# Second expert's last four batches and the global rows moved into the Strassen part of an attention and mixture-of-experts kernel

## The chip, the cores and the metric

The kernel runs on one core of a Trainium2 chip. The metric is the device time of one execution in microseconds (us). The core has TensorE (PE: matmuls, and weight loads shown apart as PEld), VectorE (DVE), ScalarE (ACT), GpSimd (POOL) and SyncE (SP); POOL and SP issue the transfers (DMAs) of this kernel, each from its own queue in order. Every engine works through its own instructions in order.

## The reference

Eight batches, eight heads, 512 local and 32 global tokens, head width 64. Global tokens attend to everything; local ones attend to the 32 global keys and to local keys at a distance of at most 32. The result (4352 rows of 512) goes through eight experts, each two matrices with a ReLU between; each row's sum over the experts is weighted with a matrix P of rows by experts, made from the gate's logits by eight Sinkhorn iterations.

```python
s_g = scale * q_g @ k_all.T ; out_g = softmax(s_g) @ v_all
s_l = concat(scale * q_l @ k_g.T, where(|i - j| <= 32, scale * q_l @ k_l.T, -1e9))
out_l = softmax(s_l) @ concat(v_g, v_l)
x = concat(out_g, out_l) as rows of 512
P = exp(x @ w_gate - max)
for _ in range(8): P /= P.sum(1) ; P /= P.sum(0) ; P *= N / E
out = sum over e of P[:, e] * (relu(x @ w1[e]) @ w2[e])
```

w1 is 512 x 1024 and w2 is 1024 x 512 for every expert. The copies of x, weights and hidden values on the chip are in 16 bits, sums in 32.

## The kernel before

The rows are kept transposed in xT, in nine groups: the local rows of batch m are group m (0 to 7, 512 rows each), the global rows of all batches are group 8 (256 rows). The program has three parts.

**Attention with two experts' work in between** (loop at L516). A step s handles one pair of heads; four steps make a batch, 32 steps all eight, and steps 32 and 33 only finish. In a step TensorE runs, in the order written out from L580 on: scores in three pieces (`st_B`, L317), transposes of the exponentials (`st_D1`, `st_D2`), transposes of the next step's keys and queries (`st_A`, L297), the product with the values of the step before (`st_E`, L375), and in even and odd steps the first and the last parts of the global rows' attention (`st_G1` to `st_G3n`). Scores go through VectorE (mask and maximum, L344) to ScalarE (exponential, L347). The transposed queries are copied by ScalarE into qbd (L314), the keys by VectorE into kTe (L307). Each step's scores need the qbd that was copied in the step before.

Between these stand pieces of the first two experts, computed plainly. A first-layer piece `p_l1` (L468) is four matmuls of 128 x 512 (for group 8 of 128 x 256) and a ReLU by ScalarE or VectorE; a second-layer piece `p_l2` (L482) is eight matmuls and a copy by ScalarE, and after the last piece of a group SP stores the group's result in yd. `f1` and `f2` in the loop take the next piece of the step's lists l1 and l2, if there is one: a first-layer piece ahead of the scores' first part, two after their second part, one at the end of the step; a second-layer piece after `st_D1`, another after `st_E`. A step has four first-layer and two second-layer pieces, experts 0 and 1 in turn for each batch:

```python
pieces = range(4 * (s - 6) + 2, 4 * (s - 6) + 6)
l1 = [(i // FT % 2, i // FT // 2, i % FT) if i >= 0 else None for i in pieces]
```

In the same loop POOL makes sums of weight blocks for experts 2 to 7, which Strassen's scheme needs: `sums_load` (L100) loads a quarter of an expert's weights into pw, `sums_form` (L108) makes four sums with four operations on 16-bit values and stores them in DRAM (kept). From step 8 on there is one load a step, its sums a step later, 24 in all. POOL also issues the loads of queries, keys (L155) and values (L170 to L177) of the next batch; when the values are there, SP moves them and the batch's global values vgz (L161) into place.

**Sinkhorn.** The pieces that the loop didn't reach stand in `tail` (L669): the second layer of expert 1 for batch 6, and experts 0 and 1 for batch 7 and for group 8. They run between the Sinkhorn iterations (`tail_run`, by weight: 1 for a first-layer piece, 2 for a second-layer one). What is left by then is mixed into the first four slots of the third part (`fill` in `run_slot`, L953).

**Experts 2 to 7 by Strassen's scheme** (from L709), with 7 instead of 8 block products in both layers. Two halves (pas 0: batches 0 to 3; pas 1: group 8 and batches 4 to 7) go through the six experts, so there are 12 stages. A stage's first layer is in slots (class `Slot`): seven products, two matmuls of 512 columns each, for each of four slots per pair of batches, and for group 8 one slot with 56 matmuls of 128 columns. The second layer is in units (class `Unit`) of 28 matmuls of 256 columns. A slot's products are interleaved with those of the previous slot and of two units (`run_slot`). ScalarE and VectorE read, copy and add the products; VectorE makes the sums of hidden values (L806) and of tokens (`token_sum`, L739). `fetch` (L711) loads an expert's weights and the stored sums, over POOL's queue. The results of experts 0 and 1 come back from yd tile by tile and VectorE adds them (`stored_load`, `stored_add`). A stage with `e == 2` writes the accumulators first, by ScalarE (L849, L864); later ones add by VectorE. The last expert's second layer for the final units is plain (L870).

Of the kernel before, what the change touches and what calls it, by code (L numbers as in the profile page):

```python
# [23 lines left out]
def kernel(  # L24
# [13 lines left out]
    nc = tc.nc  # L38
# [54 lines left out]
    work = {}  # L93

# [33 lines left out]
    with ExitStack() as att:  # L128
# [379 lines left out]
        NU = B * HP  # L508
        nc.vector.tensor_copy(out=mask[:, 0, 0:KW], in_=mask[:, 1, 0:KW])
# [6 lines left out]
        for s in range(NU + 2):  # L516
# [32 lines left out]
            if 8 <= s < 8 + 4 * (E - 2):  # L549
                sums_load(s - 8)  # L550
            if 8 < s <= 8 + 4 * (E - 2):
                sums_form(s - 9)

            l1, l2 = [], []
            if s >= 5:
                pieces = range(4 * (s - 6) + 2, 4 * (s - 6) + 6)
                l1 = [(i // FT % 2, i // FT // 2, i % FT) if i >= 0 else None for i in pieces]
            if s >= 6:
                k, hf = divmod(s - 6, 2)
                if k >= 1:  # L560
                    l2 = [((k - 1) % 2, (k - 1) // 2, 2 * hf + i) for i in range(2)]
# [107 lines left out]
        tail = [(2, lambda c=c, **k: p_l2(1, B - 2, c, "a", **k)) for c in range(NJ)]  # L669
        for e, m in ((0, B - 1), (0, B), (1, B - 1), (1, B)):  # L670
            nt = groups[m][1] // P
            tail += [(1 if nt == NJ else 0.5, lambda e=e, m=m, fm=fm, **k: p_l1(e, m, fm, "a", **k))
                     for fm in range(2 if (e, m) == (0, B - 1) else 0, FT)]
            tail += [(2, lambda e=e, m=m, c=c, **k: p_l2(e, m, c, "a", **k)) for c in range(nt)]
# [25 lines left out]
    with tc.tile_pool(name="tpool", bufs=2) as tpool, \  # L700
# [8 lines left out]
        stages = [(pas, e) for pas in range(2) for e in range(2, E)]  # L709
        w1s, w2s, sws, vws, tbs, ogs = {}, {}, {}, {}, {}, {}  # L710
        def fetch(k, l):  # L711
# [7 lines left out]
            else:  # L719
# [4 lines left out]
                own = w[:, 0:HF, H2:D]  # L724
            for o, i in parts:
                nc.gpsimd.dma_start(out=o, in_=i)  # L726
            nc.gpsimd.dma_start(out=own, in_=kept[e][l][:, 3])
            nc.gpsimd.dma_start(out=s, in_=kept[e][l][:, 0:3])

# [61 lines left out]
        class Unit:  # L791
# [54 lines left out]
            def r2(self):  # L846
                z = self.z
                if self.e == 2:
# [12 lines left out]
            def r1(self):  # L861
                z = self.z[:, 2:4, :]
                if self.e == 2:
# [89 lines left out]
        def run_slot(a, jobs=()):  # L953
# [14 lines left out]
            if x is None:  # L968
                fill(1)
# [11 lines left out]
            if y is None:  # L981
                fill(some - 1)
# [36 lines left out]
        for k, (pas, e) in enumerate(stages):  # L1019
# [4 lines left out]
            if more:  # L1024
                jobs[0 if k else 4].append(lambda: fetch(k + 1, 0))
                jobs[5].append(lambda: fetch(k + 1, 1))
            else:
                jobs[5].append(lambda: work.__setitem__("last", load_w2(e)))
            if e == 2 and pas:
                for i in range(4):  # L1030
                    jobs[1 + i].append(lambda i=i: token_sum(3, i))
            if e == E - 1 and not pas:
                for i in range(4):
                    jobs[4 + i].append(lambda i=i: token_sum(2, i))
                    jobs[4 + i].append(lambda i=i: token_sum(NQ, i))
            if e == 2:
# [53 lines left out]
```

## Time and profile before

| | |
|---|---|
| median of 3 runs | 998.37 us (997.82 to 999.82) |
| profiled execution | 998.93 us |
| its span, first to last instruction | 997.2 us |
| mean granted TensorE clock | 0.998 |
| attention loop | to about 320 us |
| Sinkhorn iterations | 327 to 357 us |
| Strassen part | from 356 us |

Busy times are unions of an engine's instructions; matmuls overlap, each is shown with the time to its last result, so the distance between starts is what one costs. A row of the timeline has start, length, engine, line, operation, output and inputs, and how many were merged; brackets show idle time of the engine ahead of it and what ended it. In DMA rows the last number is the median time from issue to landing.

### The profile page before, as it was taken

Reading aid. Unit: us, or ns where it says so; the run is one execution under the profiler, and the core shown is the slowest. Engines: PE = TensorE matmul, PEld = TensorE weight load, DVE = VectorE, ACT = ScalarE, POOL = GpSimd, SP = SyncE. Lnnn points to the kernel's source line nnn. Section 1 sums busy time; section 2 is a strip of 40 time slices with the busy share of each in tenths; the row PEclk is TensorE's granted clock in tenths of the full one; section 3 lists DMA queues with packets and bytes.
Section 4 is the critical chain, followed back from the end, with each engine's and each line's share of the span. In section 5 each row is a group of like instructions: output and inputs, shape, how many; then the busy total and the mean of one; then the engine's idle time right before and its main releaser. Section 6 shows DMA issues by size and latency. Waiting matters only on the chain.

```text
span 997.2 us, 22451 instructions
## 1 busy us (share of the span) xinstructions
PE 982.5 (99%) x8868; PEld 641.0 (64%) x8868; DVE 767.2 (77%) x1858; ACT 655.5 (66%) x1342; POOL 301.7 (30%) x364
## 2 busy tenths in 40 slices
PE   7899999999999999999999999999999999999998
PEld 4566566656665555666666666676767676776764
DVE  7866665666653755889999888997899999888885
ACT  6888888888884566765555555557765555555551
POOL 9748887888850102111111111111111111100000
PEclk9999999999999999999999999999999999999999
DMA  9999999999952387554543333575664543123043
GB/s 167 186 156 199 239 206 221 222 200 222 234 144 85 108 241 169 161 147 121 122 107 74 75 75 74 128 214 129 165 148 117 117 96 66 53 65 74 2 106 127
DMA packets 138058, 138.68 MB, mean 139 GB/s; under 512 B 56608, under 2 KB 110048, under 8 KB 135904
## 3 DMA queue, kind: packets, MB, share of 16 engines
q0 software_dynamic: 105696, 87.32, 49.6%
q1 hardware_dynamic: 31696, 49.60, 15.5%
q8 instruction: 69, 1.13, 0.5%
q10 hardware_dynamic: 560, 0.33, 0.1%
q14 instruction: 37, 0.30, 0.1%
HBM read 144.46 MB, written 39.58 MB: 185 GB/s over the span
## 4 chain that ended last, share of the span: by engine, by line
PE 94%; POOL 3%; DMA 1%; DVE 1%; issue 0%; SPq 0%; ACT 0%; POOLq 0%; DVEq 0%
PE z L810 30%; PE pa L908 18%; PE py L489 12%; PE ph L475 12%; PE pb L908 9%; PE pc L908 4%; PE po L388 1%; PE ptw L354 1%; PE zp L879 1%; PE sc L337 1%; DMA vgz<-vg 1%; PE pk L305 1%; PE tgx L364 1%; PE pq L305 1%; PE sg L407 0%; POOL va L174 0%
## 5 line engine op out<-in xcount | busy, mean ns | idle before, releaser
L810 PEld LDWEIGHTS <-hs 128*128 128x128 f16 x2264 | 220.7, 98 | 91.8 <-DVE hs L806 0.4
L810 PE MATMUL z<-w2e,hs 128*128 128x256 f16 x1304 | 195.6, 273 | 0.0
L810 PE MATMUL z<-v,hs 128*128 128x256 f16 x960 | 144.0, 273 | 0.0
L475 PE MATMUL ph<-xT,w1e 128*128 128x512 f16 (+1 forms) x576 | 129.3, 367 | 0.6 <-ACT xT L372 0.6
L347 ACT ACTIVATE Pu<-ms,mx 128x160 f16<-128x160 f32 x256 | 120.1, 636 | 13.3 <-DVE mx L344 10.4
L489 PE MATMUL py<-w2e,hT 128*128 128x512 f16 x544 | 128.2, 379 | 0.0
L831 ACT COPY z<-z 128x256 f32<-128x256 f32 x98 | 35.0, 357 | 141.7 <-PE z L810 141.7
L908 PEld LDWEIGHTS <-w1e 128*128 128x128 f16 x960 | 87.1, 98 | 51.6 <-issue 1.0
L908 PE MATMUL pa<-t,s 128*128 128x512 f16 x384 | 114.2, 379 | 0.0
L726 POOL DMA_DIRECT2D w1e<-in_moe_w_dram x24 | 17.5, 734 | 297.5 <-PE pa L908 220.4
L344 DVE CUSTOM_DVE_ANT_0 ms<-sc,mask 128x160 f32<-128x160 f32 x256 | 70.2, 320 | 46.6 <-ACT yst L492 30.0
L844 DVE SCALAR_TENSOR_TENSOR oy<-z,lg,oy 128x512 f32<-128x512 f32 x128 | 95.8, 749 | 7.6 <-ACT oy L849 5.1
L806 DVE TENSOR_TENSOR hs<-hs 128x512 f16<-128x512 f16 x224 | 94.9, 424 | 8.2
L912 DVE CUSTOM_DVE_ANT_0 hx<-pb,s 128x512 f16<-128x512 f32 x96 | 65.9, 687 | 36.4 <-ACT s L942 30.2
L726 POOL DMA_DIRECT2D w2e<-in_moe_w_dram x24 | 19.8, 833 | 243.6 <-PE z L810 214.2
L928 ACT ACTIVATE hs<-pa 128x512 f16<-128x512 f32 x96 | 57.2, 596 | 47.0 <-PE pa L908 46.9
L475 PEld LDWEIGHTS <-w1e 128*128 128x128 f16 x576 | 53.4, 98 | 52.9
L912 DVE CUSTOM_DVE_ANT_0 hs<-pb,s 128x512 f16<-128x512 f32 x96 | 65.9, 686 | 24.1 <-ACT s L942 23.7
L908 PEld LDWEIGHTS <-s 128*128 128x128 f16 x720 | 65.6, 98 | 28.5 <-issue 0.3
L489 PEld LDWEIGHTS <-hT 128*128 128x128 f16 x544 | 49.8, 98 | 51.9
L480 DVE TENSOR_SCALAR hT<-ph 128x512 f16<-128x512 f32 x58 | 40.1, 692 | 55.1 <-PE ph L475 55.0
L478 ACT ACTIVATE hT<-ph 128x512 f16<-128x512 f32 (+1 forms) x86 | 50.6, 588 | 28.8 <-PE ph L475 28.4
(197 smaller groups left out, 1971.0 us busy)
## 6 DMA issues: line engine op xcount, KB each, us to landing
ys<-yd SPq DMA_DIRECT2D x68, 256.0 KB, 3.2
yd<-yst SPq DMA_DIRECT2D x16, 1024.0 KB, 5.9
pw<-in_moe_w_dram POOLq DMA_DIRECT2D x24, 512.0 KB, 10.1
kept<-psum POOLq DMA_DIRECT2D x24, 512.0 KB, 5.3
s<-kept POOLq DMA_DIRECT2D x12, 768.0 KB, 8.9
v<-kept POOLq DMA_DIRECT2D x12, 768.0 KB, 8.9
w1e<-in_moe_w_dram POOLq DMA_DIRECT2D x12, 512.0 KB, 5.3
w2e<-in_moe_w_dram POOLq DMA_DIRECT2D x12, 512.0 KB, 6.7
```

Source lines behind the costliest of these rows:

```text
L344: nc.vector.tensor_tensor_reduce(out=ms[:, ii, :], in0=sc[:, SW * ii : SW * (ii + 1)], in1=mask[:, mi, :], scale=-scale, scalar=BIG, op0=A ...
L347: nc.scalar.activation(out=d["Pu"][:, i // 4, :, i % 4], in_=ms[:, ii, :], func=AF.Exp, scale=-1.0, bias=d["mx"][:, i : i + 1])
L475: nc.tensor.matmul(ph[:, 0:n], wts[e][0][:, dk, P * fm : P * (fm + 1)], xT[:, dk, c0 : c0 + n], start=(dk == 0), stop=(dk == DP - 1))
L478: nc.scalar.activation(out=hT[:, fm, 0:n], in_=ph[:, 0:n], func=AF.Relu)
L480: nc.vector.tensor_scalar(out=hT[:, fm, 0:n], in0=ph[:, 0:n], scalar1=0.0, scalar2=None, op0=ALU.max)
L489: nc.tensor.matmul(py, hT[:, fk, P * c : P * (c + 1)], wts[e][1][:, fk, :], start=(fk == 0), stop=(fk == FT - 1))
L806: nc.vector.tensor_tensor(out=o, in0=x, in1=y, op=op)
L810: nc.tensor.matmul(o, lhs[:, fk, :], rhs[:, fk, :], start=(first and fk == 0), stop=(fk == HF - 1), skip_group_check=True)
L844: nc.vector.scalar_tensor_tensor(out=o, in0=z, scalar=p, in1=o, op0=ALU.mult, op1=ALU.add)
L908: nc.tensor.matmul(o, lhs[:, dk, P * f : P * (f + 1)], rhs[:, dk], start=(first and n == 0 and dk == 0), stop=(dk == HD - 1), skip_group_c ...
L912: nc.vector._custom_dve(TENSOR_ADD_SAT, out=self.to(i, j), in0=self.of(ps), in1=self.of(s), s0=BIG, s1=0.0)
L928: nc.scalar.activation(out=self.to(1, 0), in_=self.of(self.pa), func=AF.Relu)
```

## The change

Expert 1 is computed plainly only for batches 0 to 3. For batches 4 to 7 and group 8 it becomes a stage of its own in the second half, ahead of expert 2, so there are 13 stages; in that half expert 1 writes the accumulators first (`inits`), and only expert 0's stored results are added there.

The loop's pieces follow a new list of (expert, batch), `seq`, at 20 first-layer pieces in 7 steps (`done`), 80 in all, and half as many second-layer pieces, shifted by 8. Where a step has two or three first-layer pieces, the second place stays empty (`l1.insert(1, None)`). The tail has the second layer of expert 0 for batch 6, expert 0 for batch 7 and group 8, and expert 1 for batch 3. In the first slots the piece that stood ahead of a slot's first unit products when there was no unit yet is no longer drawn.

POOL makes and stores the weight sums of experts 2 to 6 only, 20 instead of 24, spread over steps 8 to 31 (`sum_slots`). For experts 1 and 7 `fetch` loads each matrix whole in one transfer, and VectorE makes the sums (`weight_sums`), 8 operations a matrix, spread over slots: those of the first layer in the stage before, in slots 2 to 7, those of the second layer in slots 0 to 3 of its own. The token sums of group 8 move one stage earlier.

```diff
+    KEPT = range(2, 7)
+    sum_slots = [8 + n * 25 // 20 for n in range(4 * len(KEPT))]
...
+        seq = [(0, 0), (1, 0), (0, 1), (0, 2), (1, 1), (0, 3), (0, 4), (1, 2), (0, 5), (0, 6)]
...
-            if 8 <= s < 8 + 4 * (E - 2):
-                sums_load(s - 8)
-            if 8 < s <= 8 + 4 * (E - 2):
-                sums_form(s - 9)
-
-            l1, l2 = [], []
-            if s >= 5:
-                pieces = range(4 * (s - 6) + 2, 4 * (s - 6) + 6)
-                l1 = [(i // FT % 2, i // FT // 2, i % FT) if i >= 0 else None for i in pieces]
-            if s >= 6:
-                k, hf = divmod(s - 6, 2)
-                if k >= 1:
-                    l2 = [((k - 1) % 2, (k - 1) // 2, 2 * hf + i) for i in range(2)]
+            if s in sum_slots:
+                sums_load(sum_slots.index(s))
+            if s - 1 in sum_slots:
+                sums_form(sum_slots.index(s - 1))
+
+            def done(s):
+                c = min(max((s - 5) * 20 // 7 + 2, 0), FT * len(seq)) if s >= 5 else 0
+                return c, max((c - FT) // 2, 0)
+
+            (p1, p2), (q1, q2) = done(s - 1), done(s)
+            l1 = [(*seq[i // FT], i % FT) for i in range(p1, q1)]
+            l2 = [(*seq[i // NJ], i % NJ) for i in range(p2, q2)]
+            if s == 5:
+                l1 = [None, None] + l1
+            if 1 < len(l1) < 4:
+                l1.insert(1, None)
...
-        tail = [(2, lambda c=c, **k: p_l2(1, B - 2, c, "a", **k)) for c in range(NJ)]
-        for e, m in ((0, B - 1), (0, B), (1, B - 1), (1, B)):
+        tail = [(2, lambda c=c, **k: p_l2(0, B - 2, c, "a", **k)) for c in range(NJ)]
+        for e, m in ((0, B - 1), (0, B), (1, 3)):
...
-        stages = [(pas, e) for pas in range(2) for e in range(2, E)]
+        stages = [(pas, e) for pas in range(2) for e in range(2 - pas, E)]
+        inits = [2] * NJ + [1] * (B + 1 - NJ)
...
+            if e not in KEPT:
+                nc.gpsimd.dma_start(out=w, in_=x)
+                return
...
+        def weight_sums(k, l):
+            if l == 0:
+                w, s = w1s[k], sws[k]
+                b11, b12, b21, b22 = (w[:, HD * i : HD * (i + 1), F // 2 * j : F // 2 * (j + 1)] for i in range(2) for j in range(2))
+                ops = ((s[:, 1], b11, b12, ALU.subtract), (b12, b12, b22, ALU.add),
+                       (s[:, 0], b12, b11, ALU.subtract), (s[:, 2], b21, s[:, 0], ALU.subtract))
+                parts = [slice(i, i + 1) for i in range(HD)]
+            else:
...
+            return [lambda o=o, x=x, y=y, op=op, r=r: nc.vector.tensor_tensor(out=o[:, r], in0=x[:, r], in1=y[:, r], op=op)
+                    for o, x, y, op in ops for r in parts]
...
-                if self.e == 2:
+                if self.e == inits[self.m]:
...
             do(a, "m1")
             some = -(-len(tail) // (HF - a.f)) if tail and a is not None else 0
-            if x is None:
-                fill(1)
             if a is not None and p is None:
                 fill(1)
                 some -= 1
...
             if y is None:
-                fill(some - 1)
+                fill(some)
...
+                if stages[k + 1][1] not in KEPT:
+                    for i, at in enumerate((2, 3, 4, 5, 6, 6, 7, 7)):
+                        jobs[at].append(lambda i=i: weight_sums(k + 1, 0)[i]())
...
+            if e not in KEPT:
+                for i in range(8):
+                    jobs[i // 2].append(lambda i=i: weight_sums(k, 1)[i]())
```

## Prediction

> **What bounds the kernel now.** I read the page first (busy time per engine), then busy time by windows for two attention steps and two stretches of the second part, then the timeline of one step, engine by engine, then transfers.
>
> ```profile
> PE 982.5 (99%) x8868; PEld 641.0 (64%) x8868; DVE 767.2 (77%) x1858; ACT 655.5 (66%) x1342; POOL 301.7 (30%) x364
> ...
> 202.48:212.85 10.37, 10.37 (x139) 6.29 (x138) 6.50 (x26) 8.32 (x17) 6.81 (x7) 1.00 1.22 270
> 212.85:222.94 10.09, 10.09 (x127) 6.15 (x126) 6.16 (x26) 8.76 (x19) 9.55 (x11) 1.00 0.86 152
> 550.00:575.00 25.00, 25.00 (x174) 16.76 (x172) 20.42 (x37) 14.24 (x30) 2.72 (x4) 1.00 0.33 75
> 625.00:650.00 25.00, 25.00 (x185) 17.23 (x183) 24.30 (x54) 14.25 (x29) 3.09 (x5) 1.00 0.55 138
> ```
>
> The first line is the page's; the others are windows (length, then busy time of PE, weight loads, DVE, ACT, POOL, then clock, DMA share, GB/s). The first window is step 22 of the attention loop, the second step 23. TensorE is busy from end to end at full clock, in attention as in the second part, so the time is TensorE's list of work. But in attention ScalarE has 8.3 to 8.8 of 10 us, and around 625 VectorE has 24.3 of 25: both become the bound if TensorE gets much shorter there.
>
> **TensorE's own list.** These rows give its prices and the length of a stage.
>
> ```profile
> 205.95 1.89 PE L475 MATMUL ph<-xT,w1e 128*128 128x512 f16 x8
> ...
> 649.85 1.45 POOL L726 DMA_DIRECT2D w1e<-in_moe_w_dram  x2 [19.21 <-PE pa L908]
> 704.66 1.45 POOL L726 DMA_DIRECT2D w1e<-in_moe_w_dram  x2 [24.95 <-PE pa L908]
> ```
>
> Eight 512-column matmuls start at 205.95 and the next work at 207.67: 0.216 us each. A 256-column one takes 0.109 (four of L810 in 0.43). Removed for the second expert: per batch 32 matmuls in each layer, 4 x 64 x 0.216 = 55.3; global rows 32 x 0.109 + 16 x 0.216 = 6.9; together 62.2 us. Added: one more second-half stage. Its length is the distance between two weight fetches, 704.66 - 649.85 = 54.8 us. Balance: **-7.4 us**, if nothing waits.
>
> Of the 62.2, attention (steps 5 to 33) gives up 57.0: 34 first-layer pieces (114 to 80) of 0.864 and 16 second-layer pieces (52 to 36) of 1.73. The pieces behind the loop give up 5.2, all among those mixed into the first four slots: the Sinkhorn iterations draw about the same weight of pieces as before. What covered other engines' latency is gone there, so I walk the places.
>
> **ScalarE's turn in a step.** These ACT rows are from step 22 (its first score matmul is at 202.48); between the first two stand a global row's exponential and three copies.
>
> ```profile
> 203.39 1.37 ACT L347 ACTIVATE Pu<-ms,mx 128x160 f16<-128x160 f32 x3
> ...
> 206.79 1.39 ACT L347 ACTIVATE Pu<-ms,mx 128x160 f16<-128x160 f32 x3
> 207.90 0.70 ACT L478 ACTIVATE hT<-ph 128x512 f16<-128x512 f32 x1
> 208.84 1.01 ACT L347 ACTIVATE Pu<-ms,mx 128x160 f16<-128x160 f32 x2 [0.24 <-DVE mx L344]
> 209.60 1.28 ACT L314 COPY qbd<-pq 64x512 f16<-64x512 f16 x2
> ```
>
> The next step's first score matmul needs the last row (qbd), which ends at 209.60 + 1.28, so 8.4 us after the step's start; now TensorE comes there at 10.37, with 2 us to spare. In the changed step the ReLU at 207.90 and one piece ahead of it are gone. The exponentials of 206.79 stay at 4.31 and free ScalarE at 5.40. TensorE ends its one piece at 4.33; VectorE's ReLU on it (0.61) and the last maxima follow, so the last two exponentials start at 5.50, qbd at 6.26, and ends at 7.54. With 0.06 for the signal: ready at 7.6, in odd steps (the same walk) at 7.43. TensorE gets there, in an even step with three first-layer and one second-layer pieces, at 10.37 - 0.40 (logits) - 0.86 - 1.73 = 7.37, in an odd one at 10.09 - 2.59 = 7.49; with two first-layer pieces 0.86 earlier. By the new piece counts, from step 8: even (3,1) without logits, steps 16 and 28: 0.23 each; (2,1) in 13 and 27: 0.8 each; (2,1) in 20: 1.1; steps with two second-layer pieces or logits none. Sum **3.2 us**. Lower end 1 (if the copies' signal comes earlier by 0.2 and VectorE's ReLU later), upper end 6 (0.15 more at every one of the 16 steps with one second-layer piece).
>
> **Start of attention.** In step 6 the transposes at 47.52 wait for VectorE's copy of the step's first transposes (46.78 + 0.68), with or without the removed piece ahead of them: 0.9 of the 1.7 removed there is not gained. Then batch 2's values:
>
> ```profile
> 60.54 3.85 SPq L161 DMA_DIRECT2D vgz<-vg  x4
> ...
> vgz<-vg SPq DMA_DIRECT2D x4, 32.0 KB, 8.3
> ...
> 76.37 0.20 PE L388 MATMUL po<-vgz,pg 128*64 128x65 f16 x2
> ```
>
> The last of the four issues is at about 63.7 and lands some 9 us later, at 72.7; nothing ahead of it depends on TensorE. It is used at 76.37, which moves to 71.2 (1.73 gained in steps 6 and 7, 2.59 in step 8, 0.86 in step 9). **1.6 us** of waiting, between 0 and 3 as the landing varies. Later batches have 14 to 22 us between landing and use, and lose most of it (below).
>
> **End of attention and the first four slots.** Step 33's logits wait for the copy of xT, with 0.4 us of other work where 4 us stood: **0.4**. In slots 1 to 3 the piece between a slot's first product and the previous slot's fourth is gone (the case of no unit yet), so that product waits for the copy of pa into pre3. Slot 4 has no piece now and shows the gap:
>
> ```profile
> 379.76 0.59 PE L908 MATMUL pa<-t,s 128*128 128x512 f16 x2
> 380.19 0.59 PE L908 MATMUL pa<-xT,w1e 128*128 128x512 f16 x2
> 380.62 0.38 PE L919 MATMUL pc<-xT,identity 128*128 128x512 f16 x1
> 381.09 0.59 PE L908 MATMUL pa<-t,w1e 128*128 128x512 f16 x2
> ```
>
> From 380.19 on, 0.43 of product and 0.22 of identity cover 0.65 of about 0.9; without the identity (slots 2 and 3) 0.4 each stays open. In slot 0 the third product needs VectorE's token sums, done at 359.8, where TensorE would be at 359.1 with one piece instead of three (0.75); its last product has no piece ahead (0.4); slot 1 waits 0.2 + 0.25 and then 0.4 for a VectorE still on the second token sums to 363.1. Sum **2.8** (1.5 to 4): of 5.2 removed, 2.4 are gained.
>
> **VectorE in the second part.** 16 weight sums a stage for experts 7 (twice) and 1, each like L806 at 0.42 (0.34 back to back). A slot is 14 x 0.216 + 28 x 0.109 = 6.1 us, VectorE has 20.42/25 x 6.1 = 5.0 of it, leaving 1.1. Expert 7's stage in the first half gets 24 sums (token sums too), up to 4 a slot in its last two slots, the next stage 4 in slots 1 to 3: 1.4 to 1.7 against 1.1, a backlog of 2 us at most. Today, two stored additions a slot (1.3 against 1.1, five slots running) go through without a TensorE wait. **0.4** (0 to 2). Weights for these sums come in one transfer per layer: 1 MB took 9.4 us (w1e at 20 us); the first sum comes over 12 us after the issue, so that hides; if it took 3 us more, VectorE would stand still for them, three times. The 18 stored additions fewer in the second half, and the longer first accumulation on ScalarE, only relieve VectorE where it is not needed. POOL's queue issues one transfer for such a matrix instead of four, SP's stores five results and loads 18 tiles fewer; both queues are idle most of this part (POOL 2.72 of 25), so that is nothing.
>
> **POOL's queue and the loads.** POOL forms 20 sums in 25 steps instead of one a step, so per step its work falls about as the step does (10.1 to 8.2). Its chain today: four matrix operations of 1.16, 1.5 of issues, and a weight transfer of 7 to 12 us that is issued only one sum ahead; the value loads queue between. With these rows, values of batches 5 to 7 would land between 5 us before and 3 us after their use. I take **1.2** (0 to 6).
>
> **Sum.** -7.4 + 3.2 + 0.9 + 1.6 + 0.4 + 2.8 + 0.4 + 1.2 = +3.1 us. The profiled execution took 998.93 (span 997.2 and 1.7 around it), so 1002.0; that execution stands 0.56 above the median 998.37, hence **1001.5**. A difference under 0.2% (2 us) counts as none.
>
> **Rivals.**
> - *The cover holds.* ScalarE's copy comes in time and the landings are early: only steps 6 and the slots give back, 0.9 + 2.5. -4 us: 994.4. For it: ScalarE would have only 7.4 to 7.8 of 8.2 us; against: it stands in a chain, with the walk above. It decides if less than 5.4 us is given back.
> - *Loads fall behind.* POOL's sums and the key and value loads set the step: 20 sums at 9.9 us (24 took 58 to 295) are 198 us, the 25 shorter steps 203. If transfers also get 10% longer, the last batches are 6 to 8 us late instead of 1.2: 1007. For it: DMA share over 1.0 in most attention windows; against: bytes per step fall too.
> - *VectorE becomes the bound* around the two new stages, 24.3 of 25 already: 3 us of backlog more, 1004.5.
> - *The clock drops.* In the first 25 us TensorE was 18.96 busy and the clock 0.93: eight matmuls of L243 started 0.43 apart, half speed. If waits grow to several us, each such stretch costs about 2 us: with loads 4 us late (2.8 more than in the sum) and two such stretches, 1008. At 25 to 50, 21.8 of 25 busy, it stayed 1.00. [...]
>
> **How the numbers follow.** Forecast 0.53 (a tenth of all within 0.2%), cover holds 0.24 (0.03 within), give-back between the two 0.07 (no change), loads 0.10, VectorE 0.04, clock 0.02. Faster 0.21, within 0.20, slower 0.59. The forecast's own range is 999 to 1004.5. From 993.5 to 1008 no more than 0.15 is left out: the lower part of the cover's case (with nothing given back it would be 991) and the worst of the loads.
>
> **What would show it.** Windows of single steps: 7.4 to 8.3 us where one second-layer piece stands, with PE waits on ACT qbd in steps 13, 20, 27; a PE wait on DMA vgz near 71; slots 0 to 3 about 21.4 us instead of 23.9; the second part 54.8 longer, with PE without a gap. The forecast is wrong if the steps show no wait on qbd, or if PE waits on va, ks or vgz of batches 5 to 7 for more than 3 us.

## The result, and the profile after

The changed kernel takes **1008.84 us** (median of 6 runs, 1006.86 to 1010.72) against 998.54 of the kernel before (6 runs, 997.44 to 999.82): 1.0103 times as long, 95% interval 1.0086 to 1.0120. The forecast was 1001.5 us with a range of 993.5 to 1008.0. The direction was right, the loss of 10.3 us more than three times the forecast 3.0, and the time lies 0.8 us above the range. The profiled execution took 1006.95 us (span 1005.14, against 998.93 and 997.16 before), so it shows 8.0 of the 10.3. It lies inside the forecast's range; the median does not.

First the busy times of the page, which answer to the first line shown of before.

```profile
PE 981.0 (98%) x8984; PEld 650.0 (65%) x8984; DVE 810.2 (81%) x1963; ACT 655.1 (65%) x1353; POOL 270.1 (27%) x330
```

TensorE is busy 1.5 us less in a span 8.0 us longer: 9.5 us more of idle time. (The -7.4 us of the list can't be read off here: a matmul counts as busy to its last result, so 0.16 us of a wait of 1.06 does too, and so does work at half clock.) Where it lies is read from windows of the changed kernel (length, busy time of PE, weight loads, DVE, ACT and POOL, then granted clock, DMA share, GB/s): the wait in step 9 and what follows it, step 20, step 22, and a stretch of the second part with VectorE's new sums.

```profile
70.39:73.13 2.74, 0.19 (x7) 0.10 (x1) 1.01 (x5) 2.20 (x6) 0.00 (x0) 0.95 1.34 210
73.13:77.04 3.91, 3.88 (x40) 2.09 (x40) 2.21 (x6) 0.62 (x2) 3.25 (x3) 0.60 1.30 205
162.50:170.40 7.90, 7.00 (x119) 4.71 (x109) 5.87 (x26) 7.30 (x17) 6.52 (x7) 1.00 1.00 261
178.90:187.90 9.00, 9.00 (x128) 5.73 (x126) 6.29 (x26) 7.36 (x18) 7.90 (x9) 1.00 1.06 206
600.00:625.00 25.00, 24.98 (x210) 17.76 (x208) 24.34 (x51) 13.85 (x29) 2.72 (x4) 1.00 0.73 202
```

Steps with enough pieces (the fourth line) still keep TensorE full. Step 20, with two first-layer pieces and one second-layer piece, has a hole of 0.9. The second part is as full as before, though VectorE has 24.3 of 25 us. The first two lines are the new thing: 2.7 us of nothing, then 3.9 us at a clock of 0.60. TensorE's timeline shows both waits on the global rows' values, the one on `qbd`, and one in the slots (start, length, engine, line, operation; in brackets the idle time ahead and what ended it).

```profile
73.16 0.21 PE L390 MATMUL po<-vgz,pg 128*64 128x65 f16 x1 [2.58 <-DMA vgz<-vg]
...
74.40 2.80 PE L477 MATMUL ph<-xT,w1e 128*128 128x512 f16 x8
...
169.44 0.23 PE L339 MATMUL sc<-kTe,qbd 128*128 128x128 f16 x1 [0.90 <-ACT qbd L316]
...
210.75 0.19 PE L390 MATMUL po<-vgz,pg 128*64 128x65 f16 x1 [2.47 <-DMA vgz<-vg]
...
322.55 0.59 PE L934 MATMUL pa<-t,w1e 128*128 128x512 f16 x2 [0.30 <-ACT s L968]
```

Eight matmuls of 0.216 us should have left TensorE free 1.73 us after 74.40; the next work starts at 77.04, 2.64 after.

The timeline of POOL in the changed kernel shows the length of a stage and what stands ahead of the value loads of batch 6.

```profile
59.92 0.80 POOL L108 DMA_DIRECT2D pw<-in_moe_w_dram  x1
73.71 2.26 POOL L122 TENSOR_TENSOR psum<-pw 128x512 f16<-128x512 f16 x2 [12.99 <-DMA pw<-in_moe_w_dram]
...
185.99 0.65 POOL L172 DMA_DIRECT2D vg<-in_v_g_dram  x1
186.56 0.85 POOL L173 DMA_DIRECT2D va<-in_v_l_dram  x1
...
657.62 1.45 POOL L736 DMA_DIRECT2D w1e<-in_moe_w_dram  x2 [25.42 <-PE pa L934]
...
712.43 1.45 POOL L736 DMA_DIRECT2D w1e<-in_moe_w_dram  x2 [25.30 <-PE pa L934]
```

A stage is 712.43 - 657.62 = 54.81 us, as before. POOL stood 13 us before its first sum, waiting for the weights. The loads of the values of batch 6 belong to step 22, whose first score matmul stands at 176.95; POOL comes to them at 185.99, 9.0 us into the step. The kernel before has the same load here, and its sums waited for weights as the second row says; the third row is the changed kernel's (total, times, longest).

```profile
196.99 0.65 POOL L170 DMA_DIRECT2D vg<-in_v_g_dram  x1
POOL psum L120 <- DMA pw<-in_moe_w_dram: 37.1, 13, 14.6
POOL psum L122 <- DMA pw<-in_moe_w_dram: 44.7, 11, 13.0
```

There POOL was 5.5 us ahead of step 22, which began at 202.48. It stood still for weights in the kernel before too, 37.1 us for 24 sums; with four sums fewer in shorter steps it stands 44.7.

**The sum, term by term.** Measured in the profiled run: waits of TensorE by their places, or a step's length against the same step where the wait is absent.

| term | forecast | measured |
|---|---|---|
| TensorE's list | -7.4 | -7.4 (stage 54.81 for 54.8; the 62.2 removed are not measured apart) |
| ScalarE's turn (qbd) | 3.2 | 3.14: 0.77, 0.20, 1.06, 0.78, 0.33 in steps 13, 16, 20, 27, 28 |
| step 6 | 0.9 | 0.96 (gained 0.77 of 1.73) |
| values of batch 2, step 9 | 1.6 | 2.74 |
| half clock behind that wait | none | 1.53 |
| logits: step 33, small waits | 0.4 | 0.52 and 3 x 0.21 |
| slots 0 to 3 | 2.8 | 2.83 (21.50 us for 23.93) |
| VectorE, second part | 0.4 | 0.97, at 594 to 631 us |
| loads of batches 5 to 7 | 1.2 | 2.97, all batch 6, step 25 |

The column adds up to 8.9; the span grew by 7.98. In this execution step 6 began at 43.10 us, in that of the kernel before at 44.68, though the pieces up to there are the same. From there to the end the span grew by 9.6, of which the column leaves 0.7 without a place. In the traces of the variants below step 6 begins at 43.2 to 49.8, so this is an execution with an early start; with a later one TensorE comes later to the wait in step 9.

### The profile page after: what moved, and what is told of

It reads as the page before. It is cut to its first block, busy times and chain, and to the rows that moved or that the text cites. A ratio compares the mean times of both kernels' runs of the same rounds, so it can differ in the third digit from the quotient of the medians.

```text
span 1005.1 us, 22762 instructions
## 1 busy us (share of the span) xinstructions
PE 981.0 (98%) x8984; PEld 650.0 (65%) x8984; DVE 810.2 (81%) x1963; ACT 655.1 (65%) x1353; POOL 270.1 (27%) x330
## 3 DMA queue, kind: packets, MB, share of 16 engines
q1 hardware_dynamic: 28384, 40.16, 12.6%
q8 instruction: 70, 1.15, 0.5%
## 4 chain that ended last, share of the span: by engine, by line
PE 87%; DMA 4%; ACT 4%; DVE 3%; SPq 1%; issue 1%; POOL 0%; ACTq 0%; DVEq 0%
PE z L836 33%; PE pa L934 19%; PE pb L934 10%; PE py L491 7%; PE ph L477 6%; PE pc L934 5%; DMA vgz<-vg 2%; ACT Pu L349 2%; DMA va<-in_v_l_dram 1%; PE zp L905 1%; PE ptw L356 1%; PE po L390 1%; PE sc L339 1%; DMA yd<-yst 1%; DVE ms L346 1%
## 5 line engine op out<-in xcount | busy, mean ns | idle before, releaser
L836 PEld LDWEIGHTS <-hs 128*128 128x128 f16 x2468 | 239.9, 98 | 101.4 <-DVE hs L832 2.6
L836 PE MATMUL z<-w2e,hs 128*128 128x256 f16 x1420 | 213.0, 273 | 0.0
L836 PE MATMUL z<-v,hs 128*128 128x256 f16 x1048 | 157.3, 273 | 0.0
L934 PEld LDWEIGHTS <-w1e 128*128 128x128 f16 x1056 | 95.4, 98 | 57.9 <-issue 3.1
L934 PE MATMUL pa<-t,s 128*128 128x512 f16 x416 | 123.8, 379 | 0.5 <-DVE t L775 0.3
L477 PE MATMUL ph<-xT,w1e 128*128 128x512 f16 (+1 forms) x416 | 97.6, 373 | 0.6 <-ACT xT L374 0.6
L491 PE MATMUL py<-w2e,hT 128*128 128x512 f16 x400 | 94.1, 379 | 0.0
L968 ACT COPY s<-pa 128x512 f32<-128x512 f32 x111 | 65.1, 586 | 13.1 <-PE pa L934 0.7
L959 ACT COPY s<-pa 128x512 f32<-128x512 f32 x111 | 65.1, 586 | 12.9 <-PE pa L934 1.4
L934 PE MATMUL pb<-xT,s 128*128 128x512 f16 (+1 forms) x264 | 66.1, 345 | 0.4 <-DVE hx L938 0.4
L934 PE MATMUL pc<-xT,w1e 128*128 128x512 f16 (+1 forms) x264 | 66.1, 345 | 0.1
```

Source lines behind the costliest of these rows:

```text
L477: nc.tensor.matmul(ph[:, 0:n], wts[e][0][:, dk, P * fm : P * (fm + 1)], xT[:, dk, c0 : c0 + n], start=(dk == 0), stop=(dk == DP - 1))
L491: nc.tensor.matmul(py, hT[:, fk, P * c : P * (c + 1)], wts[e][1][:, fk, :], start=(fk == 0), stop=(fk == FT - 1))
L836: nc.tensor.matmul(o, lhs[:, fk, :], rhs[:, fk, :], start=(first and fk == 0), stop=(fk == HF - 1), skip_group_check=True)
L934: nc.tensor.matmul(o, lhs[:, dk, P * f : P * (f + 1)], rhs[:, dk], start=(first and n == 0 and dk == 0), stop=(dk == HD - 1), skip_group_c ...
L959: nc.scalar.copy(out=self.pre2, in_=self.pa)
L968: nc.scalar.copy(out=self.pre3, in_=self.pa)
```

## The experiments

One theory stood at the start, with two rivals. *Late values*: the loss beyond the forecast is the fetching of the global rows' values, which stands behind the moves of `vb` on SP and behind POOL's sums, and doesn't move when TensorE gets faster; the other terms are as forecast. Against it: that transfers set the pace of attention in general, so that a cured wait comes back at the next tile, and that VectorE's new sums are the cause. Each kernel below changes only what its diff shows. The before-kernel's median beside them was 998.83 to 999.02.

### e1: values early

```diff
 def first():
-    nc.gpsimd.dma_start(out=vg16[b], in_=v_g[b]...)
+    if b < 2:
+        load_vg(b)
 ...
 def move():
 ...
-    if b > 1:
-        load_vz(b)
 ...
+if hp == 1 and b:
+    load_vg(b + 1)
 if hp == 2:
+    if b:
+        load_vz(b + 1)
     *loads, move = load_v(b + 1)
```

> The changed kernel, with the values of the global rows for batches 2 to 7 fetched ahead: the cast copy vg16 is issued one step earlier on POOL, and the five loads of vgz and vgn stand on SP one step earlier, ahead of the three vb moves instead of behind them. Nothing else differs. Theory (late values): the two TensorE waits on vgz (2.7 us in step 9, 3.0 us in step 25) go, and with the first of them the half clock behind it (about 1.5 us); the waits on qbd (3.1 in all) and slots 0 to 3 (2.8) stay. So 1008.8 - 7.2 = 1001.6 us (1000 to 1003). If late landings are also what spreads the runs, the runs lie within 2 us of each other instead of 4. Rival (POOL's sums and the load of the transfers set the pace of attention): the next thing is late instead, TensorE waits on vb, va or ks of batches 2 and 5 to 7 and less than 3 us is gained, 1006 to 1008. Rival (VectorE with the weight sums in the second part): no more than 1 us is gained in attention.

Measured: **1001.37 us** (8 runs, 1000.61 to 1002.70), 1.0024 times the kernel before (1.0012 to 1.0035): 7.5 us less than the changed kernel, where 7.2 was expected. Step 9 takes 7.93 us instead of 12.20, step 25 7.93 instead of 10.93, all other steps are as they were, within 0.1 us from step 7 on. First the largest TensorE waits of this run (total, times, longest), then SP's timeline.

```profile
PE sc L341 <- ACT qbd L318: 2.1, 3, 0.9
PE pk L309 <- DVE pw L360: 1.7, 3, 1.0
```

```profile
50.56 2.86 SPq L163 DMA_DIRECT2D vgz<-vg  x4
53.51 0.58 SPq L164 DMA_DIRECT2D vgn<-vg  x1
55.40 0.60 SPq L197 DMA_DIRECT2D vb<-va  x1
```

No wait on a transfer is left among the large ones. Issued from 50.6 on, the four loads of batch 2 land 2.6 to 3.8 us later; issued from 60.8 on in the changed kernel, behind SP's wait for `va`, and with a weight matrix of 1 MB, two loads of 512 KB and four of 256 KB issued in the 6 us ahead of them, they took 8.0 to 9.9. The runs now spread over 2.1 us instead of 3.9. Late values cost 7.5 of the 10.3 us. That the figure was met so nearly is in part luck: the 7.2 was read from the profiled execution and subtracted from the median of all runs. Between the two profiled executions the two steps gain 7.27, but the span only 5.65, because step 6 begins 1.43 us later in this one (44.53 for 43.10).

### e4: the same edit in the kernel before

The diff is that of e1.

> The kernel before, with the same edit of the fetching of the global rows' values. There TensorE never waits for them, so the theory expects no change: 998.5 us, within 0.6. If the edit alone gained 3 us or more here, it would be a gain of its own that has nothing to do with the change, and the comparison with the first run would have to be made against this one.

Measured: 998.92 us (10 runs, 997.41 to 1000.37), 0.9997 times before (0.9986 to 1.0007). The edit has no gain of its own; it only undoes what the change brought.

### e2 and e3: half of qbd by VectorE

```diff
-nc.scalar.copy(out=qb[r, :, HB * a : HB * (a + 1)]..., in_=...)
+(nc.vector.tensor_copy if a else nc.scalar.copy)(
+    out=qb[r, :, HB * a : HB * (a + 1)]..., in_=...)
```

> The changed kernel, with one of the two qbd copies of each step (the half of head a = 1) by VectorE instead of ScalarE, from step 6 on. Theory: the five waits on qbd (0.77, 0.20, 1.06, 0.78, 0.33 us in steps 13, 16, 20, 27, 28) go, since ScalarE's chain is 0.64 us shorter and VectorE has 1.5 us of slack in a step. But the 2.0 us of these that stand ahead of step 25 come back there, because the values of batch 6 land at a time that TensorE doesn't set: only the 1.1 us behind it are gained, about 1007.7 us (1006.5 to 1008.5). Rival (the landing moves along with TensorE's steps): all 3.1 us are gained, 1005.7. Rival (VectorE is the tighter engine already): new TensorE waits on VectorE's copies and 1009 or more.

e3 is e1 and e2 together:

> Both edits together: values fetched ahead, and one of the two qbd copies by VectorE. Theory: with no late values the turn's waits are gained in full: 1008.8 - 7.2 - 3.1 = 998.5 us (997 to 1000), which is about the kernel before; what is then left against the list's -7.4 us is step 6 (0.9), the first slots (2.8), step 33 and the logits (1) and VectorE in the second part (1). Rival (transfers set the pace): waits on vb, va or ks appear, 1003 or more.

Measured: e2 1016.63 us (5 runs, 1.0187 times before, 1.0169 to 1.0204), e3 1016.63 (4 runs, 1.0176, 1.0163 to 1.0190). Both theories missed, the rival of a tighter VectorE was right in its sign. The instructions of that line in e2 (ns, least/median/most) with what they waited for, and e2's largest TensorE waits:

```profile
L316 ACT COPY qbd<-pq x26: 570/683/704, 40.8 to 262.4; 64x512 f16<-64x512 f16 x26
L316 DVE COPY qbd<-pq x26: 694/695/695, 41.4 to 263.1; 64x512 f16<-64x512 f16 x26
...
  ACT qbd L316: 25.3, 26
```

```profile
PE sc L340 <- DVE qbd L316: 4.7, 6, 1.3
PE sg L410 <- DVE xn L396: 4.4, 8, 0.6
PE py L492 <- DVE hT L483: 2.4, 6, 0.4
```

VectorE's half starts only when ScalarE's half has ended: all 26 waited for it, 25.3 us in all, standing on VectorE's queue ahead of the next `xn` and ReLU. So the copy was not shared, it was put in a row over two engines, and a step that TensorE had filled (7.93 us) took 8.6. That e3 gains nothing over e2 fits late values: with steps that long, TensorE comes to the values after they have landed.

### e11: without the empty place

```diff
-if 1 < len(l1) < 4:
-    l1.insert(1, None)
```

> The changed kernel without the empty place that it puts second in a step's list of two or three first-layer pieces: a second piece then stands in the middle of the step with its ReLU on ScalarE, and none is left for the step's end. Theory (ScalarE's turn is what a short step waits for): its chain gets 0.70 us of ReLU back while TensorE loses the piece that covers the end, so the waits on qbd rise from 3.1 to 10 us or more and stand in most steps with one second-layer piece: about 1015 us (1012 to 1019). Rival (ScalarE's turn is no limit, the waits come from elsewhere): 1008 to 1010.

Measured: **1011.69 us** (4 runs, 1011.21 to 1011.94), 1.0130 times before (1.0117 to 1.0144), 2.9 above the changed kernel. The largest TensorE wait, and ScalarE's timeline in step 20:

```profile
PE sc L339 <- ACT qbd L316: 10.2, 14, 1.4
```

```profile
168.65 1.41 ACT L349 ACTIVATE Pu<-ms,mx 128x160 f16<-128x160 f32 x3
169.78 0.70 ACT L480 ACTIVATE hT<-ph 128x512 f16<-128x512 f32 x1
170.36 1.01 ACT L349 ACTIVATE Pu<-ms,mx 128x160 f16<-128x160 f32 x2
171.10 1.29 ACT L316 COPY qbd<-pq 64x512 f16<-64x512 f16 x2
```

The ReLU stands between the exponentials again, and the waits on `qbd` rise from 3.1 to 12.7 us (by the distances between TensorE's starts, less the matmuls' own; the row counts from the modelled end of the matmul ahead). The mechanism is the expected one; the edit does two things at once, the ReLU in the chain and no piece at the step's end, and this run doesn't part them. The time is below the expected 1012 to 1019 because steps 9 and 25 wait for no values any more: 12.7 - 3.1 - 7.3 = 2.3 more than the changed kernel, 2.9 measured. Time lost in one of the two places is not lost in the other.

### e6: pieces evened out

On e1:

```diff
-return c, max((c - FT) // 2, 0)
+return c - (s in (12, 26)), max((c - FT) // 2, 0) + {15: -1, 19: -1, 28: 1}.get(s, 0)
```

> The changed kernel with early values (as in e1), and the same pieces in the same order spread more evenly: step 13 and 27 take one first-layer piece from the step ahead of each, 16 and 20 one second-layer piece from the step ahead, and 28 one from the step behind, so that no step has less than 7.8 us of TensorE work. Theory (a step can't be shorter than ScalarE's turn, 7.2 us from even to odd and 7.9 from odd to even): the five waits on qbd (3.1 us) go and nothing takes their place, since the work is the same: 1001.4 - 3.1 = 998.3 us (997.5 to 999.2). Rival (the turn is a matter of the whole chain through ScalarE and VectorE, and longer steps push it too): waits of the same sum appear at other steps, 1000.5 to 1001.5.

Measured: 999.78 us (12 runs, 997.92 to 1007.69), 1.0019 times before (1.0003 to 1.0036). Between the two expectations, and with a new spread. In the profiled execution (1003.12) no wait on `qbd` is left, and step 25 takes 13.04 us instead of 7.93; its largest TensorE wait and the windows of that wait and of what follows:

```profile
PE po L392 <- DMA vb<-va: 3.3, 1, 3.3
```

```profile
202.63:206.10 3.47, 0.18 (x7) 0.04 (x1) 1.25 (x6) 2.45 (x6) 3.31 (x4) 1.00 1.10 333
206.10:210.36 4.26, 4.23 (x49) 2.31 (x50) 2.21 (x6) 0.61 (x2) 3.96 (x6) 0.60 1.17 253
```

The turn's theory holds: with one piece more in each of the five short steps their waits are gone. But TensorE is now 2.5 us earlier at batch 6, and next in line is the move of `vb`, which comes behind the `va` loads that POOL issued at 184.2. It costs 3.5 us and half clock after it (0.60 in the mean), 5.1 in all; 1003.12 - 5.1 = 998.0 is close to the forecast 998.3. Six of the twelve runs lie above 1000; whether by the same wait, no trace says. So the rival of the transfers has its part: it is the next limit, about 2 us behind.

### e9: sums formed a step later

On the changed kernel, without e1:

```diff
+if s - 2 in sum_slots:
+    sums_form(sum_slots.index(s - 2))
 if s in sum_slots:
     sums_load(sum_slots.index(s))
-if s - 1 in sum_slots:
-    sums_form(sum_slots.index(s - 1))
```

> The changed kernel (its values fetched as it does, behind the vb moves), but with each of POOL's weight sums formed two steps behind its load instead of one, and ahead of that step's load. Theory (POOL stands in front of the values' loads, waiting for a weight transfer): the loads of va for batch 6 are issued at 186 us, 9 us into their step, because POOL waits for pw and forms four sums first; with the weights already there they are issued several us earlier and all behind them too, so the wait on vgz of batch 6 (3.0 us) goes, while batch 2, whose loads lie ahead of the first sum, keeps its 2.7 and the half clock behind it: 1008.8 - 3.0 = 1005.8 us (1005 to 1006.7). Rival (the transfers themselves are slow, whenever they are issued): the wait stays within 1 us of what it was, 1008 to 1009.5.

Measured: **1001.66 us** (5 runs, 1001.39 to 1002.39), 1.0032 times before (1.0020 to 1.0044): 7.2 us gained, where 3.0 was expected. POOL's timeline at the first load of batch 6, and what its sums waited for in the whole run:

```profile
172.49 0.63 POOL L172 DMA_DIRECT2D vg<-in_v_g_dram  x1
```

```profile
POOL psum L122 <- DMA pw<-in_moe_w_dram: 23.1, 9, 5.6
```

POOL waits 23.1 us for weights instead of 44.7, comes to batch 6's values at 172.5, 2.1 us ahead of step 22 (174.62) instead of 9.0 behind its start, and step 25 takes 7.93. That part is shown. The wait on batch 2 is absent too, which the edit doesn't explain in full: in this execution TensorE reached step 9 1.9 us later (67.45 for 65.52 at its Pu transposes, after a start of attention that took 2.0 us longer), and the last of the four loads landed at 72.2 instead of 73.1, just in time. Whether the runs without a trace lost that wait in the same way, or had a larger one on batch 6 in the changed kernel, is open. A third place for it is batch 1's values, which no edit here moves: TensorE waited for them in step 5, 1.9 us in e12's profiled execution and 3.1 in e5's. The longer runs of the changed kernel had the lower granted clock: 0.992 to 0.995 in the four runs above 1008 us, 0.996 in the two of 1006.9.

### e7: halved pieces in the first slots

On e1; `p_l2` gets an argument that gives out four of its eight matmuls:

```diff
+halved = None
+if x is None and y is None and p is not None and a is not None and tail:
+    halved = tail.pop(0)[1]
+    halved(pool=ps_z, tag="z", half=0)
 do(x, "m4", "m5", "r2", "r7")
 do(p, "m4")
 ...
 if y is None:
-    fill(some)
+    if halved:
+        halved(half=1)
+    else:
+        fill(some)
```

> The changed kernel with early values (as in e1); the one second-layer piece that each of slots 1 to 3 has is given out in two halves of four matmuls, one ahead of the previous slot's fourth product, as cover for the copy into pre3, the other where the piece stands now. Theory: the waits of 0.40 to 0.46 us on pre3 in slots 1 to 3 go (1.1 to 1.3 in all), those of slot 0 and slot 4 (1.4) stay: 1001.4 - 1.2 = 1000.2 us (999.7 to 1000.8). Rival (the halved piece leaves the wait behind it uncovered): a wait on pre2 ahead of the last product of each slot, and no gain.

Measured: 999.83 us (12 runs, 998.60 to 1003.07), 1.0004 times before (0.9994 to 1.0014): 1.5 less than e1. TensorE's timeline at the same place as the last row shown of the changed kernel:

```profile
319.59 0.59 PE L944 MATMUL pa<-xT,w1e 128*128 128x512 f16 x2
320.02 1.03 PE L495 MATMUL py<-w2e,hT 128*128 128x512 f16 x4
320.88 0.59 PE L944 MATMUL pa<-t,w1e 128*128 128x512 f16 x2
```

Four matmuls now stand where TensorE waited for the copy into `pre3`, and slots 1 to 3 are 0.86, 0.48 and 0.48 us shorter. What exceeds the expected 1.1 to 1.3 is in slot 1, where e1 also has a wait of 0.36 on VectorE that is gone here. No new wait on `pre2` appeared.

### e8: the weight sums by POOL

On e1:

```diff
-... nc.vector.tensor_tensor(out=o[:, r], in0=x[:, r], in1=y[:, r], op=op)
+... nc.gpsimd.tensor_tensor(out=o[:, r], in0=x[:, r], in1=y[:, r], op=op)
```

> The changed kernel with early values (as in e1), and all 48 weight sums of the second part by POOL instead of VectorE. POOL takes 1.16 us for such an operation of one matrix quarter and stands idle 80% of these stages, so sixteen sums are about 10 to 19 us of a stage of 48 to 55. Theory: the 1.0 us in which TensorE waits for VectorE at 603 to 628 us goes, and nothing else changes: 1000.4 us (1000.0 to 1001.0). Rival (POOL beside VectorE takes time from it, or the sums come late): TensorE waits on VectorE or on the sums, 1002 or more.

Measured: **1044.38 us** (5 runs, 1039.35 to 1046.17), 1.0433 times before (1.0410 to 1.0456). VectorE's and POOL's timelines at one of the places:

```profile
623.16 11.45 DVE L838 TENSOR_TENSOR hs<-hs 128x512 f16<-128x512 f16 x4
```

```profile
624.44 2.29 POOL L759 TENSOR_TENSOR v<-w2e 128x512 f16<-128x512 f16 x2
626.66 2.27 POOL L759 TENSOR_TENSOR w2e<-w2e 128x512 f16<-128x512 f16 x2
628.87 2.26 POOL L759 TENSOR_TENSOR v<-w2e 128x512 f16<-128x512 f16 x2
631.08 2.25 POOL L759 TENSOR_TENSOR v<-w2e,v 128x512 f16<-128x512 f16 x2
```

Four sums of VectorE, 0.43 us each where POOL is idle, take 11.45 here; one of them took 10.0, as long as POOL's eight sums in a row with a little around them. TensorE stands 9.2 us for it, and the granted clock from 624 to 635 us is 0.64 in the mean, in the whole run 0.98; the second part is 45 us longer. The rival was right, far beyond its figure. Slots 50 and 51, each 0.27 us longer in the changed kernel than the same slots before, are again as long as before: those 0.54 us are VectorE's sums for expert 1's second layer.

### e5: the wait filled

On the changed kernel; eleven extra matmuls whose result nobody reads:

```diff
+if s == 9:
+    keep_busy(11)
 if 3 <= s <= NU:
     st_E(s - 1)
```

> The changed kernel, with eleven extra 512-column matmuls whose result nobody reads, put right ahead of the attention-weighted sums of step 9, where TensorE waits 2.7 us for the values of batch 2. Theory (an idle TensorE loses its clock): the extra work fills 11 x 0.216 = 2.4 us of the wait, the values land when they did, and the eight matmuls behind take 1.73 us instead of 2.64, the sums 0.033 each instead of 0.05: step 9 takes about 10.7 us instead of 12.2, and the kernel 1007.3 instead of 1008.8 us. Rival (the slow stretch is something else, the copies of vb or the landing itself): step 9 stays at 12.2 us or longer, the matmuls behind still take 2.6 us, and the time is 1008.8 or up to 2.4 above. If the values land earlier than 2.4 us after TensorE comes there, the extra work costs the difference.

Measured: 1010.76 us (4 runs, 1009.63 to 1011.26), 1.0114 times before (1.0101 to 1.0127). It decides nothing. In its profiled execution the values of batch 1 were late in step 5 (14.48 us instead of 8.41), so TensorE came to step 9 6.8 us later, when batch 2's values were there, and the extra work only made step 9 longer (10.53 us for 7.93). Whether filling the wait would have kept the clock stays open.

### e10: all cures together

e1, e6, e7 and e9, and the last batch's logits behind two more pieces:

```diff
-logits(NJ * (B - 1), NJ, ps_sc, "sc")
 ...
 tail_run(2)
+logits(NJ * (B - 1), NJ, ps_po, "po")
 st_G4(1)
```

> The changed kernel with all the edits that took a wait away: values early (e1), pieces evened out (e6), sums formed two steps behind their load (e9), halved pieces in slots 1 to 3 (e7), and the logits of the last batch behind two more pieces instead of right behind the copy that they need. Theory: what is left against the list's -7.4 us is step 6 (0.9), the logits' small waits (0.6), slots 0 and 4 (1.0) and VectorE in the second part (1.0): 1001.4 - 3.1 - 1.5 - 0.5 = 996.3 us (995.3 to 997.3), 2.5 us faster than the kernel before. Rival (the moves of vb are late again, as in the run of e6 that was profiled): a wait on vb of 3 us or more in step 25, 998 to 1001.

Measured: **996.28 us** (9 runs, 994.80 to 997.13), **0.9973** times before (0.9964 to 0.9982): a version that beats both kernels, by 2.6 and 12.6 us. The expected 996.3 was met. Its largest TensorE waits:

```profile
PE pk L309 <- DVE pw L360: 1.7, 3, 1.0
PE pt L236 <- DVE kTe L311: 1.4, 3, 0.7
PE sc L338 <- ACT qpl L314: 1.3, 1, 1.3
```

All three belong to the first eight steps; the kernel before has the last two alike and the first with 0.7. Neither `vgz`, `vb` nor `qbd` is among the waits above 0.4 us. By the terms left (0.96, 0.63, 1.0 and 0.97) against -7.4 it would be 3.8 below the kernel before. The profiled executions differ by 4.1 (spans 993.0 and 997.2), but 1.45 of that lies ahead of step 6 (43.23 and 44.68); from there on it is 2.7, as the medians say (2.6). So the gain is 1.1 smaller than the terms give, and where that goes is open.

### e12: all 24 sums by POOL in attention

e10, and:

```diff
-KEPT = range(2, 7)
-sum_slots = [8 + n * 25 // 20 for n in range(4 * len(KEPT))]
+KEPT = range(2, 8)
+sum_slots = [8 + n * 25 // 24 for n in range(4 * len(KEPT))]
```

> As e10, but with expert 7's weight sums formed by POOL in attention too, as in the kernel before (24 sums, one a step), so that VectorE forms only those of expert 1 (one stage instead of three). Theory: TensorE's waits for VectorE in the second part fall from 1.0 to 0.5 us or less, and with the sums formed two steps behind their load POOL still issues the values in time: 995.7 us (994.8 to 996.8). Rival (POOL's load in the shorter steps): waits on vb, va or vgz come back, 998 or more.

Measured: 995.80 us (9 runs, 994.75 to 998.24), 0.9971 times before (0.9960 to 0.9982), no different from e10. From slot 4 to the plain part both take 654.49 us, so the forecast gain in the second part did not come: expert 7's two stages of sums cost TensorE nothing on VectorE, and the 0.97 stays, around the stage of expert 1, whose sums e12 leaves where they are. Nor did four sums more in attention bring late loads back: the one large wait for a transfer, 1.9 us on `vgz`, is that of batch 1 in step 5, ahead of the first sum.

## Why the forecast was right, and where it was not

The direction and most terms were right. What failed is the price of late values: the two terms for batch 2's values and for POOL's loads stood at 2.8 in the sum, and the profiled execution lost 7.24 there; taking these waits away (e1) gives back 7.5 of the 10.3 us.

- **TensorE's list, -7.4.** Right for the stage, 54.81 us; e10 shows a gain once the waits are gone, 2.6 us of the 3.8 that the list less the waits left would give.
- **ScalarE's turn, 3.2.** Right in size (3.14) and in its steps (13, 16, 20, 27, 28), and in its mechanism by e11, where the ReLU put back in the chain and the missing piece at the end bring 12.7, and e6, where fuller steps bring none. The walk let TensorE go on 7.6 us after the start of an even step; in step 20 it started at 161.86 and went on at 169.44, 7.58 later.
- **Step 6, 0.9; step 33, 0.4; slots, 2.8.** Right: 0.96, 0.52 and 2.83. The slots' waits are the ones walked through, and e7 takes those on `pre3` away by the cover that the forecast named as missing. The three small waits of the logits (0.63) were not in the sum.
- **VectorE in the second part, 0.4.** Too small (0.97), in the places that the working named: 0.4 at the end of expert 7's first stage, where expert 1's first-layer sums and the token sums meet, and in the slot behind it, and 0.27 in each of slots 50 and 51 of the next stage. e8 shows the latter two to be the sums; the former is argued.
- **The wait for batch 2's values, 1.6 (0 to 3).** The place, the step and the tile were right. The landing was put at 72.7 and came at 73.1, while TensorE came at 70.4 instead of 71.2. The latter is chance: step 6 began 1.58 us earlier than in the execution that the forecast was read from; without that TensorE would have come at 72.0, by an estimate from these numbers. What failed is that the term was priced as the wait alone: the 1.5 us of half clock behind it stood only in a rival of 0.02, with the condition of several us. In this run it came with a single idle stretch of 2.58 us.
- **POOL's queue and the loads of batches 5 to 7, 1.2 (0 to 6).** The chain was named rightly, a weight transfer issued only one sum ahead with the value loads between. The step that failed is "per step its work falls about as the step does": that counts POOL's own work, but the weight transfer that POOL stands still for took about as long as before (8.0 to 12.7 us from issue to landing around batch 6, 9.4 to 12.3 in the kernel before), while the steps fell from 10 to about 8. So POOL came to batch 6's values 9.0 us into step 22 instead of 5.5 ahead of it. The result was 2.97 us instead of 1.2 in the profiled run, all at batch 6. e9 shows the mechanism by letting the weights land first. How the loss of the other runs is shared between this place and batch 2 is open. The rival *loads fall behind* had this mechanism at 0.10 and 1007.
- **The range.** Batch 2's wait came close to its upper end (2.74 of 3) and the half clock stood outside it; the loads' 2.97 lay in the middle of theirs. The two are one thing, a landing that TensorE doesn't move, where time gained ahead is given back; the range treated them as two.

## What to carry to other kernels

Before a list of work is shortened, note for each transfer when it lands and what it waits for: a landing that hangs on other queues stays where it is, and what is gained ahead of it, by cures of other waits too, can be lost again there until it is moved (e11; in e6 5.1 us at the move of `vb`). Price such a wait with what follows it, here 1.53 us of half clock. A queue whose head waits for a transfer holds all that stands behind it (POOL stood 44.7 us for weights and came to batch 6's values 9.0 us into their step), so issue the loads with a due time ahead of the wait, or give that wait a step more. Moving work to an idle engine is no gift, if its instructions hold up the neighbour's (e8, 11.45 us for four sums of 0.43) or the pieces run in a row (e2, 25.3 us of waiting on VectorE's queue): look at the duration of the neighbour's instructions, not at idle shares.

## What the runs showed of the hardware

- **Half clock after a single wait, and not always.** In the traces of the two kernels the granted clock changes only at instants a multiple of 3.41 us apart: at 10.81, 14.23 and 997.27 us in the kernel before, at 11.40, 14.82, 72.84, 76.26 and 1004.68 in the changed one. There it was half only once between the first 15 us and the last one, from 72.84 to 76.26. These are windows cut at such instants around the waits of steps 9 and 25 (first number behind the length: busy time of TensorE; third from the end: clock).

```profile
69.43:72.84 3.41, 1.15 (x32) 0.99 (x31) 1.97 (x8) 3.16 (x8) 0.00 (x0) 1.00 1.34 210
72.84:76.26 3.42, 3.10 (x36) 1.79 (x36) 1.52 (x5) 0.58 (x2) 2.47 (x3) 0.50 1.36 205
205.96:209.37 3.41, 2.31 (x46) 1.69 (x44) 2.55 (x12) 3.38 (x9) 3.25 (x4) 1.00 1.47 206
209.37:212.79 3.42, 1.87 (x37) 1.22 (x37) 1.06 (x4) 1.04 (x3) 3.12 (x5) 1.00 1.06 366
```

  In step 9 one window was left with 1.15 us of work, and the next had half the clock. The 3.0 us of step 25 are two waits, 2.47 and 0.17 us idle, and lie across two windows with 2.31 and 1.87 us of work; no half clock followed. In e6 (3.31 us idle) the window ahead of the half clock held 0.25 us of work, in e5 (0.65 and 2.48 idle) 1.12. Behind the first 15 us, in the traces of the two kernels, only that window with 1.15 us of work and the last of each execution (0.07 and 0.00) were followed by half clock; those next in work, with 1.87 and 2.31 us in the changed kernel and 2.31 in the kernel before, were followed by full clock. So in these traces where a wait falls counted as well as how long it was.
- **VectorE's sums beside POOL's.** In e8 single sums of hidden values on VectorE (128 x 512 in 16 bits) took 6.6 and 10.0 us, in e1, which differs only in the engine of the weight sums, 0.43 at most. The 6.6 lasted as long as five of POOL's sums that followed one another (5.6 us), the 10.0 as long as eight (8.9 us), where one takes 1.15. How POOL's sums hold VectorE's up is not shown.
- **Small transfers behind large ones.** The 32 KB loads of batch 2 landed 2.6 to 3.8 us after their issue in e1, and 8.0 to 9.9 us in the changed kernel, where 3 MB of other loads had been issued in the 6 us ahead. That these are the reason is not tested by itself.
